# Gated mix of block attention and an MLP: another order of the attention steps, PV groups in pairs on one PSUM tile, and three small moves

## The chip, the cores and the metric

The kernel runs on one core of one Trainium2 chip. The metric is the device time of one execution in microseconds (us). A core has five engines with an instruction queue each: TensorE (PE in the profile, with its weight loads as PEld), VectorE (DVE), ScalarE (ACT), GpSimd (POOL) and SyncE (SP). An engine takes its instructions in the order of its queue and waits at an instruction until the semaphores that it names have been raised by other engines. DMAs are issued here by SP and by ACT, each from its own queue.

## The reference

The function mixes two branches of the same input by a gate per row. S is 2048, D is 512; there are 32 heads of 16 columns; row i sees the keys i-255 to i.

```python
def _A_ref(x, wqkv, wo):                       # H = 32, Dh = 16, W = 256
    q, k, v = split_heads(x @ wqkv)
    scores = jnp.einsum("bhqd,bhkd->bhqk", q, k) * (Dh ** -0.5)
    mask = (idx[:, None] - idx[None, :] >= 0) & (idx[:, None] - idx[None, :] < W)
    p = _softmax(jnp.where(mask[None, None], scores, -1e9), axis=-1)
    o = jnp.einsum("bhqk,bhkd->bhqd", p, v)
    return merge_heads(o) @ wo

def _B_ref(x, w1, b1, w2, b2):                 # F = 1792
    y = _layernorm(x, axis=-1)
    h = _gelu(jnp.einsum("bsd,df->bsf", y, w1) + b1)
    return jnp.einsum("bsf,fd->bsd", h, w2) + b2

x = A_x
g = _sigmoid((x * gate_w).sum(-1, keepdims=True))
return g * _A_ref(x, A_wqkv, A_wo) + (1 - g) * _B_ref(x, B_w1, B_b1, B_w2, B_b2)
```

## The kernel before

Almost every product is made of a high and a low part of each operand (a rounded copy, and what is left after subtracting it): high by high, low by high, high by low. `copy` (L130) makes the high part on ScalarE, `lo_part` (L127) subtracts on VectorE unless told otherwise. The kernel has three stages.

**Projections.** `load_x` (L232) brings four pieces of 512 rows of the transposed input and makes both parts; the piece is c, its four quarters are dt. For the last piece (c = 3) the low parts are made by GpSimd (L250). `qk_unit` (L297) and `v_unit` (L326) make queries, keys and values on TensorE, with twelve matmuls for a unit. Some dozen score steps are done here already, ahead of the attention stage.

**Attention and the first MLP layer, mixed.** The heads are taken in eight groups p of four heads. The program of this stage is written as a string, `ORDER`, of one letter for each step, which `run` (L735) reads:

- `S` (`s_pair`, L348): scores of 128 queries against up to 384 keys for two heads, into a PSUM tile; VectorE masks (L366) and takes the maximum of each row (L367).
- `T` (`st_pair`, L403): the same scores transposed, with the maximum taken off inside the product; ScalarE applies exp (L414), GpSimd cuts the two triangles (L416).
- `P` (`pv`, L423): probabilities times values for 256 queries and four heads, 32 matmul instructions, or 16 for the first of a group p. Here a "full" and a "short" PV group. The sum is copied out of PSUM by ScalarE (`copy`, L441), or by VectorE (L439) once no `S` is left.
- `f` (`fill`, L706): one step of the first MLP layer, a pair of matmuls that run side by side (L638). 24 steps are a unit, whose two halves ScalarE then copies out (`out_half`, L647).

These steps share four PSUM tiles of 128x2x512, b0 to b3, which are handed round: `two` (L112) takes the tile that has been free longest, or another one where the string `PICK` says so. A step that takes a tile waits until the last reader of the tile's previous user has finished.

Every fourth block of queries `put_max` (L371) sends the row maxima through DRAM: GpSimd splits them (step 6 after the last `S`), VectorE transposes them (step 13), `put` stores them to DRAM (step 19, issued by ScalarE; while the projections still run, by SP), and `rest` loads them into the queries' rows (step 28, by SP).

**Second MLP layer and output.** `mlp2(c, f)` (L851) multiplies one of 14 blocks f of the hidden layer for one of four pieces c of rows: 12 matmuls in four groups, one for each 128 rows. Its operand is loaded six items ahead (`load_h`, L689), GELU is applied by ScalarE two items ahead, and VectorE splits it one item ahead (`parts`, L696). `attn_out(c)` (L794) is started at item (0, 4) for c = 0 and at (c-1, 11) for the others: it loads the sums of the softmax, inverts them (`inv`, L809), loads them spread out, and in its later steps scales the attention output (`scale(b)`, b = 0 to 3, VectorE L816, ScalarE, VectorE); one step after each scaling, 12 matmuls apply `wo` (`mm`, L827). `after(k, fn)` (L136) puts a function k items later, at the head of that item.

Of the kernel before, what the change touches and what calls it, by code (L numbers as in the profile page):

```python
# [34 lines left out]
EPS = 1e-5  # L35
NEG = -3.0e38
U8 = mybir.dt.uint8
ORDER = ("TfSfSfffffTfSfffTSfffTfSfffTSfffTfSffSPTSffTfSfffTSfffSPSTfSfffTfSfTffTffTSffTfffTSPSSTPSTfTfffTSffT"
         "ffSffTSffffTSfffTfSffTfSfffSPSTSPTffSTffTfffTfSTffffTSffTfSfffTSfffTfSffSPSSTPTffTSffTffSffTfSfffTSf"
         "ffTfSfffTSfffTfSfSPSTTPTTSPSSTPSffTSffffSTfffTffSffTfSfffTfSffTfSfffSPSTTffffSTffTfffSTffTfffSSPfSfT"  # L40
         "ffSffTfTfffTSPSSTPTffTSfffTfSffTfSffffTSfffTfSffTffSffTPfSSPTffSfTfSffTfSfTffTffSTfffSffTfSfffTSfffS"
         "PTSTPSTSPTffTSffTffSffTSffffTSffffSTfffTffTfSfSfPSSTPfSfTfSfffTfTffSfTfSffffTSfffTfSffffTfSPSTSPTfSf"
         "ffTSfffTfSffTfSfffTfSfTfffTSfTffffTSPTTSPSTSPfTfSTfffSfffTSfffTfSffTfSfffTSfffTfSffSPPSTffTfffSTffTf"
         "ffTfSTfffSfTffTfSffTfSfffSPSSTPSffTfSfffTSfffTfSfffTSfffTfSfffTSffffSPPfSTfTfffSfTffTfSffTffTfSffTff"
         "SfTfTffffSPTTSPSTSPSfffTSfffTfSffTfSffffTSfffTfSffTfSfffSPfSTfTffffTfSTfffTfSfffTSfffTfSffTfSfffSPTS"
         "SPPTSTffffTfSTfffSffTfSfffTSfffTfSffTfffSfSPTSTPSSfTffffTfSffTfSfffTSfffTfSfffTSfffffSTPTTSPTSffTffS"
         "ffTfSfffTSfffTffSfTfTfffSTfTfffSPSSSPPSTSffffTfSfffTSfffTfTfffSTfffTffSTffffSPSTSPSTffTfffSTffTffTSf"
         "ffSffTSfffTfSffTfSfffSPSTSPfTfSTfffTffTSfffTfSfffTSfffTfSffTfSfffSPTTSPSTSPTffTSffTfSfffTfSfffSSfffT"
         "ffffTSffTfSffSPSffTSfffTfSffTfSffSTfffTffTffTfTffffTfPPTTTPfTffTffTffTPPTfTfffTffTfffTTffTfffTfPfTTf"
         "TTffffP")  # L50
PICK = ("0000000000000000001000000000000000000001000100100000000000000000100001000100000000000001000000000000"
        "0000000000000100010000010000000000001001001000101010001000100000000000000000001000000000100000000000"
        "0010000000000001000010020101010000000000100101000000000000000010000001000010000000000000000100100010"
        "1000000000100000000000000000000000000000000000000001000000000000000000010001000000000000001000000100"
        "0000000000000000100000000000000000000000000001001100000010010000000010010000000010000010000000000010"
        "00010000000000000000000101000100000100000000000000010000000000000000000000000000000")
LAG = 6
CHAIN = (6, 13, 19, 28)

# [2 lines left out]
def gated_mix_kernel(ctx, tc: tile.TileContext, xt, x2, wq0, wqk, wv, wo, xa, gw, w1, w2, b1, b2, out):  # L62
    nc = tc.nc
    dve, act, pool, pe, sp = nc.vector, nc.scalar, nc.gpsimd, nc.tensor, nc.sync
# [5 lines left out]
    def nm(s):  # L70
        uid[0] += 1
        return f"{s}_{uid[0]}"
# [30 lines left out]
    def ps(tag, shape=(128, 512)):  # L103
        key, bufs = banks[tag]
        return left[key].tile(list(shape), F32, name=nm("ps_" + tag), tag=tag, bufs=bufs)

    ring, picks = [], list(PICK)

    def choose():
        return ring.pop(int(picks.pop(0)) if picks else 0)  # L110

    def two():  # L112
        if not ring:
            return ps("x", (128, 2, 512))
        ring.append(choose())
        return ps(ring[-1], (128, 2, 512))

    def small(tag, bufs, shape, dt=F32):
        return consts.tile(list(shape), dt, name=nm(tag), tag=tag, bufs=bufs)

    def view(t, *ap, off=0):
        return bass.AP(tensor=t.tensor, offset=t.offset + off, ap=[list(x) for x in ap])

    def f32(t):
        return t.bitcast(F32)

    def lo_part(lo, src, hi, eng=dve):  # L127
        eng.tensor_tensor(out=lo, in0=src, in1=f32(hi), op=ALU.subtract)  # L128

    def copy(dst, src):  # L130
        act.activation(dst, src, AF.Copy)  # L131
# [4 lines left out]
    def after(k, fn):  # L136
        todo.setdefault(step[0] + k, []).append(fn)
# [6 lines left out]
    spot = [None]  # L144
    soons = {}

    def soon(n, fn):
        soons.setdefault(spot[0] + n, []).append(fn)
# [32 lines left out]
    def x8():  # L181
        return get("x", "x8", 10, (128, 2048), F32R)
# [49 lines left out]
    def load_x(c):  # L232
        h, l = x8(), x8()
        xh.append(h)
        xl.append(l)
        raw = vs[:, 4 * c:4 * c + 4].rearrange("p b r -> p (b r)")
        for dt in range(DT):
            sp.dma_start(raw[:, dt * C:(dt + 1) * C], xt[c, :, dt * C:(dt + 1) * C])

        def part(t, dt):  # L240
            return t[:, dt * C:(dt + 1) * C]

        def hi(dt, eng=act):
            if eng is dve:
                dve.tensor_copy(part(h, dt), part(raw, dt))
            else:
                copy(part(h, dt), part(raw, dt))

        def lo(dt):
            lo_part(part(l, dt), part(raw, dt), part(h, dt), dve if c < 3 else pool)  # L250

        def rest():
            for dt in range(DT):
                hi(dt)
                lo(dt)

        return rest, hi, lo
# [113 lines left out]
    def put_max(p, a):  # L371
        mx = mxs[p][:, :, :, a:a + 4]
        m = small("nm", 2, (128, 2, 2, 2, 4), F32R)
        ms = small("ms", 2, (128, 32))
        md = dram.tile([2, 2, 2, 4, 128], F32R, name=nm("md"))

        def parts():
            pool.tensor_copy(m[:, 0], mx)
            lo_part(m[:, 1], mx, m[:, 0], pool)

        def turn():
            dve.transpose(ms, f32(m).rearrange("p a b c d -> p (a b c d)"))

        def put(eng=act):
            eng.dma_start(f32(view(md, [32, 4], [128, 32], [1, 32])), ms)

        def rest():
            done.add(("m", p, a // 4))
            for k in range(2):
                src = view(md, [512, 2], [1024, 2], [1, 512], off=2048 * k)  # L390
                sp.dma_start(f32(qk[62 + k:113 + k:50, :2, a * 128:a * 128 + 512]), f32(src))

        if spot[0] is None:
            parts()
            after(1, lambda: (turn(), put(sp)))
            after(3, rest)
        else:
            for n, fn in zip(CHAIN, (parts, turn, put, rest)):
                soon(n, fn)
# [19 lines left out]
    def flush():  # L419
        while late:  # L420
            late.pop(0)()

    def pv(p, j, last):  # L423
        flush()
        a = two()[:, 0]
        parts = ((-1, 0, 128, 256), (-2, 0, 256, 128), (0, 0, 0, 256), (1, 128, 0, 128))[0 if j else 2:]
        for n, (d, at, fr, w) in enumerate(parts):
            kb = 2 * j + d
            for h in range(4):
                v = (4 * p + h) * VW  # L430
                pe.matmul(a[32 * h:32 * h + 32, at:at + w], vs[:, kb, v:v + 32], pts[p, kb][:, h, fr:fr + w],  # L431
                          start=n == 0, stop=n == len(parts) - 1, skip_group_check=True, tile_position=(0, 32 * h))
        if j % 2 == 0:
            sums.append(sums.pop(0))
            acc[p] = sums[-1]
        s = acc[p]
        o = j % 2 * 256
        if last:
            dve.tensor_copy(s[:, o:o + 256], a[:, :256])  # L439
        else:  # L440
            copy(s[:, o:o + 256], a[:, :256])  # L441
        if j % 2:
            to = osc[p, :, (j - 1) * 256:(j + 1) * 256]
            if lt:
                after(1, lambda: sp.dma_start(to, s))
            else:
                act.dma_start(to, s)
# [287 lines left out]
    def run(order):  # L735
        for a in order:
            spot[0] += 1
            for fn in soons.pop(spot[0], []):
                fn()
            flush()  # L740
            if a == "T":
                p, kb, pr = lt.pop(0)
                if not pr:
                    block(p, kb)
                st_pair(p, kb, pr)
            elif a == "S":
                s_pair(*ls.pop(0))
            elif a == "P":
                pv(*lp.pop(0), not ls)
            else:  # L750
                fill()

    run(ORDER + 6 * "f")
    flush()
# [10 lines left out]
    t = spare[0]  # L765
# [28 lines left out]
    def attn_out(c):  # L794
# [5 lines left out]
        o = get("work", "oa", 2, (128, 4, 512))  # L800
        r = get("work", "ra", 2, (128, 4, 512))
# [42 lines left out]
                after(g, lambda g=g: load_o(g))  # L844
            after(4 + g, lambda g=g: load_r(g))
        for b in range(4):
            after(10 + b, lambda b=b: scale(b, *(t[:, :, b * 128:b * 128 + 128] for t in (o, r))))

    accs = {}

# [30 lines left out]
    for n in range(len(seq)):  # L881
        tick()
        for k in (n + 6,):
            c, f = item(k)
# [4 lines left out]
        c, f = item(n + 1)  # L889
# [6 lines left out]
        c, f = seq[n]  # L896
# [52 lines left out]
```

## Time and profile before

| what | us |
|---|---|
| median of three timed executions | 694.88 |
| lowest and highest of the three | 691.83 and 695.27 |
| the profiled execution, its own time | 691.57 |
| its span, first to last instruction | 689.8 |
| projections (about) | 0 to 144 |
| attention with the first MLP layer (about) | 144 to 488.5 |
| second MLP layer and output (about) | 488.5 to 689.8 |

In the page, a group of instructions stands with its line, its engine, what it writes and reads, how many there are, their busy time and the mean of one. The timeline gives for each piece its start, its length, its engine and, in brackets, how long the engine sat idle before it and who ended that. TensorE's matmuls overlap, so that the end of one lies behind the start of the next: the time that a matmul costs is the distance from its start to the next start, not its length, and a short stall may not show as idle time at all.

### The profile page before, as it was taken

Reading aid. Unit: us, or ns where it says so; the run is one execution under the profiler, and the core shown is the slowest. Engines: PE = TensorE matmul, PEld = TensorE weight load, DVE = VectorE, ACT = ScalarE, POOL = GpSimd, SP = SyncE. Lnnn points to the kernel's source line nnn. Section 1 sums busy time; section 2 is a strip of 40 time slices with the busy share of each in tenths; the row PEclk is TensorE's granted clock in tenths of the full one; section 3 lists DMA queues with packets and bytes.
Section 4 is the critical chain, followed back from the end, with each engine's and each line's share of the span. In section 5 each row is a group of like instructions: output and inputs, shape, how many; then the busy total and the mean of one; then the engine's idle time right before and its main releaser. Section 6 shows DMA issues by size and latency. Waiting matters only on the chain.

```text
span 689.8 us, 15777 instructions
## 1 busy us (share of the span) xinstructions
PE 681.9 (99%) x5738; PEld 538.2 (78%) x5738; DVE 474.1 (69%) x971; ACT 385.5 (56%) x639; POOL 267.2 (39%) x623
## 2 busy tenths in 40 slices
PE   9999999999999999999999999999999999999997
PEld 6887777877877778778787877777787888888886
DVE  6646789966877878778587777866575555556444
ACT  6437454447677676876767767678633224123221
POOL 6900156426566664755666655558000000000000
PEclk9999999999999999999999999999999999999999
DMA  8998888785765668665776556436775450841801
GB/s 319 351 317 271 246 255 270 226 248 176 231 202 165 203 212 271 194 198 177 198 251 195 182 166 202 154 108 216 277 241 189 143 181 4 267 133 40 255 0 62
DMA packets 89621, 137.92 MB, mean 200 GB/s; under 512 B 13160, under 2 KB 36648, under 8 KB 89416
## 3 DMA queue, kind: packets, MB, share of 16 engines
q1 hardware_dynamic: 81120, 128.69, 58.4%
q10 hardware_dynamic: 8424, 8.23, 3.9%
q8 instruction: 46, 0.75, 0.5%
q14 instruction: 31, 0.25, 0.1%
HBM read 81.53 MB, written 54.30 MB: 197 GB/s over the span
## 4 chain that ended last, share of the span: by engine, by line
PE 86%; DMA 7%; POOL 3%; DVE 1%; ACT 1%; SPq 1%; issue 1%; ACTq 0%; DVEq 0%; POOLq 0%
PE ps_b L638 22%; PE ps_a L858 16%; PE ps_b L431 12%; PE ps_d L303 10%; PE ps_b L357 7%; PE ps_b L412 6%; PE ps_o L827 6%; PE ps_d L333 6%; DMA ra<-rd 1%; DMA hp<-t 1%; DMA t<-in_w 1%; DMA oa<-osc 1%; PE ps_x L357 1%; DMA wv<-in_wq 1%; POOL x L128 1%
## 5 line engine op out<-in xcount | busy, mean ns | idle before, releaser
L638 PE MATMUL ps_b<-x,w 64*128 64x512 f32 x1344 | 211.1, 395 | 0.2 <-ACT pb L414 0.2
L858 PE MATMUL ps_a<-x,t 128*128 128x512 f32 x648 | 149.6, 389 | 0.0
L367 DVE TENSOR_REDUCE mx<-ps_b 128x2 f32<-128x512 f32 x208 | 144.1, 693 | 7.2
L858 PEld LDWEIGHTS ps_a<-x,t 128*128 128x128 f32 x648 | 121.6, 188 | 25.3
L638 PEld LDWEIGHTS ps_b<-x,w 64*128 64x128 f32 x1344 | 130.0, 186 | 10.6 <-issue 2.0
L366 DVE COPY_PREDICATED ps_b<-tri,ps_b 128x256 f32<-128x256 uint8 x208 | 88.3, 424 | 44.0 <-PE ps_b L357 32.7
L416 POOL TENSOR_SCALAR_AFFINE_SELECT pa<-pa 128x256 f32<-128x256 f32 x192 | 73.9, 412 | 68.6 <-ACT pa L414 67.9
L414 ACT ACTIVATE pa<-ps_b 128x768 f32<-128x768 f32 x96 | 76.5, 813 | 25.6 <-PE ps_b L412 18.8
L412 PE MATMUL ps_b<-qk 64*128 64x384 f32 (+5 forms) x512 | 88.8, 336 | 0.4 <-ACT pb L414 0.3
L303 PE MATMUL ps_d<-x,w 128*128 128x512 f32 x360 | 85.1, 391 | 0.1
L357 PE MATMUL ps_b<-qk 62*128 62x384 f32 (+3 forms) x472 | 83.2, 345 | 0.8 <-ACT t L131 0.6
L303 PEld LDWEIGHTS ps_d<-x,w 128*128 128x128 f32 x360 | 67.2, 188 | 15.1 <-POOL x L128 0.5
L416 POOL TENSOR_SCALAR_AFFINE_SELECT pb<-pb 128x256 f32<-128x256 f32 x160 | 62.4, 417 | 39.2 <-ACT pb L414 38.5
L414 ACT ACTIVATE pb<-ps_b 128x768 f32<-128x768 f32 (+2 forms) x96 | 65.6, 706 | 16.8 <-PE ps_b L412 12.5
L412 PEld LDWEIGHTS ps_b<-qk 64*128 64x128 f32 (+1 forms) x512 | 50.8, 184 | 15.7 <-issue 4.0
L694 ACT ACTIVATE t<-t,b1s 128x512 f32<-128x512 f32 x56 | 38.5, 716 | 43.4 <-DMA t<-hp 42.8
L416 POOL TENSOR_SCALAR_AFFINE_SELECT x<-x 128x256 f32<-128x256 f32 x128 | 49.7, 417 | 25.8 <-ACT x L414 25.4
L357 PEld LDWEIGHTS ps_b<-qk 62*128 62x128 f32 (+1 forms) x472 | 45.4, 184 | 17.4 <-issue 3.8
L414 ACT ACTIVATE x<-ps_b 128x768 f32<-128x768 f32 x64 | 51.2, 813 | 13.0 <-PE ps_b L412 10.4
L827 PE MATMUL ps_o<-w,t 128*128 128x512 f32 x192 | 46.3, 390 | 1.0 <-ACT t L131 1.0
L333 PE MATMUL ps_d<-wv,x 128*128 128x512 f32 x192 | 46.7, 394 | 0.0
L431 PE MATMUL ps_b<-pa,v 128*32 128x256 f32 (+1 forms) x768 | 43.3, 330 | 0.2 <-POOL x L416 0.2
(96 smaller groups left out, 757.1 us busy)
## 6 DMA issues: line engine op xcount, KB each, us to landing
qk<-qk SPq DMA_DIRECT2D x112, 196.0 KB
t<-hp SPq DMA_DIRECT2D x56, 256.0 KB
hp<-t SPq DMA_DIRECT2D x54, 256.0 KB
qk<-t SPq DMA_DIRECT2D x48, 256.0 KB
osc<-x SPq DMA_DIRECT2D x31, 256.0 KB
t<-in_w SPq DMA_DIRECT2D x28, 256.0 KB
w<-w SPq DMA_DIRECT2D x28, 256.0 KB
qk<-t ACTq DMA_DIRECT2D x24, 256.0 KB
```

Source lines behind the costliest of these rows:

```text
L303: pe.matmul(o, a[:, dt * 128:(dt + 1) * 128], b[:, dt * C:(dt + 1) * C], start=n == 0, stop=n == 11)
L333: pe.matmul(o, x[:, a:a + 128], wvs[dt][:, k], start=n == 0, stop=n == 11)
L357: pe.matmul(o[:, e, :n], qs[pr][r:k, qb * 128:qb * 128 + 128], ks[pr][r:k, t0:t0 + n], start=True, stop=True)
L366: dve.copy_predicated(o[:, :, :128], tri, o[:, :, 256:384])
L367: dve.tensor_reduce(m, o[:, :, :256], mybir.AxisListType.X, ALU.max)
L412: pe.matmul(o[:, e, :w], ks[pr][r:k, kb * 128:kb * 128 + 128], qs[pr][r:k, kb * 128:kb * 128 + w], start=True, stop=True)
L414: act.activation(pt[:, :, :w], o[:, :, :w], AF.Exp, scale=0.25)
L416: pool.affine_select(out=pt[:, :, a:a + 128], in_=pt[:, :, a:a + 128], pattern=[[0, 2], [sgn, 128]], base=b, channel_multiplier=-sgn, comp ...
L431: pe.matmul(a[32 * h:32 * h + 32, at:at + w], vs[:, kb, v:v + 32], pts[p, kb][:, h, fr:fr + w], start=n == 0, stop=n == len(parts) - 1, sk ...
L638: pe.matmul(o[:, e], w[kt // 4][r:r + 64, k, m:m + 128], y[r:r + 64, a:a + C], start=n == 0, stop=n == 23)
L827: pe.matmul(a, x[:, g], wos[g][:, k], start=n == 0, stop=n == 11)
L858: pe.matmul(accs[c][b], x[:, b * 128:(b + 1) * 128], w, start=f == 0 and n == 0, stop=f == FT - 1 and n == 2)
```

## The change

Five things are changed together. The strings `ORDER` and `PICK` are new: the same steps in another order, most of them within a few places of where they were, with the last hundred steps rearranged more. In `pv`, two `P` that follow each other directly now use the two halves of one PSUM tile, where each used to take a tile of its own; any other step closes the pair. The low parts of the last two quarters of the last input piece are made by VectorE instead of GpSimd. The scaling of the first output piece starts 12 items after its start instead of 10. In `put_max`, the stores of the first 99 steps are issued by SP instead of ScalarE.

```diff
-ORDER = ("TfSfSfffffTfSfffTSfffTfSfffTSfffTfSffSPTSffTfSfffTSfffSPSTfSfffTfSfTffTffTSffTfffTSPSSTPSTfTfffTSffT"
+ORDER = ("TfSfSfffffTSffffTSfffTfSfffTSfffTfSffSPTSffTSffTfSffTffSffSPSTfffTSffTffTfSfTfffTfSPSTSPSTfTfffTSfff"
...
         def lo(dt):
-            lo_part(part(l, dt), part(raw, dt), part(h, dt), dve if c < 3 else pool)
+            lo_part(part(l, dt), part(raw, dt), part(h, dt), dve if c < 3 or dt > 1 else pool)
...
-        def put(eng=act):
-            eng.dma_start(f32(view(md, [32, 4], [128, 32], [1, 32])), ms)
+        def put(eng=None):
+            (eng or (act if spot[0] > 99 else sp)).dma_start(f32(view(md, [32, 4], [128, 32], [1, 32])), ms)
...
+    pair = [None]
+
     def pv(p, j, last):
         flush()
-        a = two()[:, 0]
+        if pair[0] is None:
+            pair[0] = two()
+            a = pair[0][:, 0]
+        else:
+            a = pair[0][:, 1]
+            pair[0] = None
...
             flush()
+            if a != "P":
+                pair[0] = None
             if a == "T":
...
-            after(10 + b, lambda b=b: scale(b, *(t[:, :, b * 128:b * 128 + 128] for t in (o, r))))
+            after((10 if c else 12) + b, lambda b=b: scale(b, *(t[:, :, b * 128:b * 128 + 128] for t in (o, r))))
```

The string `ORDER` has 1207 letters before and 1202 after; the five `f` that it lacks follow behind the last `P`. Places where two `P` stand side by side: six before, seven after. Four instructions change their queue besides the two low parts: two stores of maxima go from ACT to SP, and two stores of hidden blocks (`hp<-t`), near the end of the stage, from SP to ACT.

The built programs show where instructions now stand. **TensorE, two PV groups side by side** (steps 584 and 585 in both). Before, the first group writes tile b3 and the second b1; a name's first number is the tile's, the rows are the end of the first group and the start of the second:

```order
L431 MATMUL ps_b3_670_4356<-pa_255_1523,v_4_80 32x128 [waits Pool_49]
L431 MATMUL ps_b3_670_4356<-pa_255_1523,v_4_80 32x128
L431 MATMUL ps_b1_671_4374<-pa_255_1523,v_4_80 32x256 [waits DVE_49,PE_49]
L431 MATMUL ps_b1_671_4374<-pa_255_1523,v_4_80 32x256
L431 MATMUL ps_b1_671_4374<-pa_255_1523,v_4_80 32x256 [waits Pool_49]
```

The same place of the changed program:

```order
L438 MATMUL ps_b0_669_4355<-pa_255_1523,v_4_80 32x128 [waits Pool_49]
L438 MATMUL ps_b0_669_4355<-pa_255_1523,v_4_80 32x128
L438 MATMUL ps_b0_669_4355<-pa_255_1523,v_4_80 32x256 [waits Activation_49]
L438 MATMUL ps_b0_669_4355<-pa_255_1523,v_4_80 32x256
L438 MATMUL ps_b0_669_4355<-pa_255_1523,v_4_80 32x256 [waits Pool_49]
```

Both groups now write the tile b0_669. The second group's first matmul used to wait for VectorE, the last reader of what had been in b1 before; now it waits for ScalarE. By the count that the semaphore must have reached, the instruction waited for is the copy of the first group's sum out of this same tile. So it is in all seven places: five wait for a copy on ScalarE, the last two for one on VectorE.

**ScalarE, the first store of maxima of this stage.** Before (pa and x8 are probabilities, t copies of a finished first-layer unit, md the maxima in DRAM):

```order
L414 ACTIVATE x8_253_1521<-ps_b0_273_1624 128x768
L414 ACTIVATE x8_253_1521<-ps_b3_275_1642 128x768
L385 DMA md_270_1593<-ms_269_1592 4x32x32
L131 ACTIVATE t_277_1660<-ps_b1_261_1536 128x512
L131 ACTIVATE t_278_1662<-ps_b1_261_1536 128x512
L131 ACTIVATE x8_253_1521<-ps_b3_280_1669 128x256
```

After:

```order
L414 ACTIVATE x8_253_1521<-ps_b0_273_1624 128x768
L414 ACTIVATE x8_253_1521<-ps_b3_275_1642 128x768
L131 ACTIVATE t_277_1660<-ps_b1_261_1536 128x512
L131 ACTIVATE t_278_1662<-ps_b1_261_1536 128x512
L131 ACTIVATE x8_253_1521<-ps_b3_280_1669 128x256
```

The store is gone from between the exponentials and the copies of the unit; it stands in SP's queue now.

**TensorE, the first product with `wo`.** Before, it follows the first item of piece c = 1 (written to ps_a_1185 to 1188 with the weights x_1056):

```order
L858 MATMUL ps_a_1187_7877<-x_1056_7104,t_7837 128x512
L858 MATMUL ps_a_1188_7878<-x_1056_7104,t_7836 128x512 x2
L858 MATMUL ps_a_1188_7878<-x_1056_7104,t_7837 128x512
L827 MATMUL ps_o_1191_7897<-w_7303,t_7863 128x512
L827 MATMUL ps_o_1191_7897<-w_7306,t_7863 128x512
```

After (the same four sums are ps_a_1176 to 1179; x_1059 are the weights of the third and fourth item):

```order
L867 MATMUL ps_a_1179_7866<-x_1048_7072,t_7859 128x512
L867 MATMUL ps_a_1176_7863<-x_1059_7161,t_7882 128x512 x2
L867 MATMUL ps_a_1176_7863<-x_1059_7161,t_7883 128x512
L867 MATMUL ps_a_1177_7864<-x_1059_7161,t_7882 128x512 x2
L867 MATMUL ps_a_1177_7864<-x_1059_7161,t_7883 128x512
L867 MATMUL ps_a_1178_7865<-x_1059_7161,t_7882 128x512 x2
L867 MATMUL ps_a_1178_7865<-x_1059_7161,t_7883 128x512
L867 MATMUL ps_a_1179_7866<-x_1059_7161,t_7882 128x512 x2
L867 MATMUL ps_a_1179_7866<-x_1059_7161,t_7883 128x512
L836 MATMUL ps_o_1190_7930<-w_7291,t_7900 128x512
```

Three items of piece c = 1 now stand ahead of the first product with `wo`, where one did.

More of the change, by code (lines that the diff above doesn't have):

```diff
@@ L37 @@
 U8 = mybir.dt.uint8
-ORDER = ("TfSfSfffffTfSfffTSfffTfSfffTSfffTfSffSPTSffTfSfffTSfffSPSTfSfffTfSfTffTffTSffTfffTSPSSTPSTfTfffTSffT"
[L39 to L56, printed above, removed]
+ORDER = ("TfSfSfffffTSffffTSfffTfSfffTSfffTfSffSPTSffTSffTfSffTffSffSPSTfffTSffTffTfSfTfffTfSPSTSPSTfTfffTSfff"
+         "TfSffTfSfffTSfffTfSffTfSfffSPSTSPTffSTffTfffTfSTffffTSffTfSfffTSfffTfSffSPSSTPTffTSffTffSffTfSfffTSf"
+         "ffTfSfffTSfffTfSfSPTSTPTTSPSSTPSffTSffffSTffffTfSffTfSfffTSfffTfSfffSPSTTffffSTfffTffSTffTfffSSPfSfT"
+         "ffSffTfTfffTSPSSTPTffTSffTffSffTfSfffTSfffTfSffTfSffTffSfSPPSTffTfSffTffTSfffTffSfTffSffTfSfffTSfffS"
+         "PTSTPSSTPTffTSffTffSffTfSfffTSfffTfSfffTTfffSfSfPSSTPfTffSTfTffSffTfSfffTSfffTfSfffSTffffTfSPSTSPfTf"
+         "SffTfSfffTSfffTfSfffSfTffTfSfTfffTfSPTSTPSSTPSffTSfffTfTffSfTffSfffTSffffTSfffTffSfSPPTSffSffTffTfff"
+         "STffTfffTfSTffTfSffTfSfffSPSSTPfTfSfffTSfffTfSffTfSfffTSffffSTffffSfSPPfSTfTfffSfTffTfSffTffSffTfffT"
+         "SffTfffTfSPTSTPSSTPSffTfSfffTfSffTfSffffTSfffTfSffTfSfffSPfSTfTffffTfSTfffTfSfffTSfffTfSffTfSfffSPTS"
+         "SPPTSTffffTfSTfffSffTfSfffTSfffTfSffTfffSfSPTSTPSSfTffffTfSffTfSfffTSfffTfSfffSTfffffTSPTTSPTSffTffS"
+         "ffTSffffTSfffTffSfTfTfffSTfTfffSPSSSPPSfTSffffTSfffTfSffTffTffSTfffTffSTffffSPSTSPSTffTfffSTffTffTSf"
+         "ffSffTfSffTfSffTfSfffSPSTSPTffSTffTfffTSffTffSffTSffffTSfffTfSfffSPTSTPSSTPTffTSffTfSfffTfSfffTSfffT"
+         "fSffTfSffTSfffSPSffTSffffTSfffTfSffSfTfffTffTffTPfTfTTffPPTfTfTfffTffTfPfTTPTfTffTfTffTffffTPPTfTfTf"
+         "fT")
@@ new lines @@
+PICK = ("0000000000000000001000000000000000000001001000100000000000000000100001000100000000000001000000000000"
+        "0000000000000100010000010000000000001001001000101010001000100000000000000000000000000000000000000000"
+        "0010000000000000000100201001000000000100100101000000000000000100000001000000010000000000000100100010"
+        "0000000010000000000001000000000000000000010000000100000000000000000010001000000000000000000001000000"
+        "0000000000001000000000100100000000000000010011000000000000000001001000000001000001000000000001000010"
+        "000000000000000000201000100000000000000000000001000000000000000000000000000")
```

## The prediction

> **What bounds the kernel now.** I read the page's busy times first, then the busy time by stage, then the timeline at the places that the change touches.
>
> ```profile
> PE 681.9 (99%) x5738; PEld 538.2 (78%) x5738; DVE 474.1 (69%) x971; ACT 385.5 (56%) x639; POOL 267.2 (39%) x623
> 0.00:143.00 143.00, 141.50 (x619) 110.30 (x620) 103.36 (x196) 73.00 (x157) 57.55 (x71) 1.00 0.87 281
> 143.00:490.00 347.00, 345.48 (x4264) 267.12 (x4263) 261.36 (x589) 250.85 (x386) 209.69 (x552) 1.00 0.62 196
> 490.00:690.00 200.00, 194.94 (x859) 160.77 (x857) 109.36 (x187) 61.62 (x97) 0.00 (x0) 1.00 0.46 148
> ```
>
> The stage rows give length, then the busy time of PE, PEld, DVE, ACT and POOL, and the granted clock. TensorE is the bound in all three stages, at clock 1.00; the next engine, VectorE, is busy 261 of 347 us in the middle one. The change adds or removes no matmul. So what it can move is TensorE's stalls: each microsecond in which it waits is on the path, and work on any other engine counts only through such a wait. What the page calls idle time of TensorE is only about 8 us of the span, since ends are modelled; I measure a stall from start to start. The sum below is made against the profiled execution, 691.57 us (span 689.8 and 1.8 around it), which lies 3.3 under the median of the timed three.
>
> **Pairs of PV groups: a new wait, seven times.** The second group of a pair now waits until the first one's sum is copied out of the shared tile. How long that is, the six old pairs show, where nothing had to wait:
>
> ```profile
> 305.98 0.86 PE L431 MATMUL ps_b<-pb,v 128*32 128x256 f32 x16
> 306.65 1.48 PE L431 MATMUL ps_b<-pa,v 128*32 128x256 f32 x32
> 307.55 0.38 ACT L131 ACTIVATE x<-ps_b 128x256 f32<-128x256 f32 x1 [0.57 <-PE ps_b L431]
> 308.71 0.44 PE L357 MATMUL ps_b<-qk 62*128 62x384 f32 x2
> 328.97 1.51 PE L431 MATMUL ps_b<-pa,v 128*32 128x256 f32 x32
> 329.95 0.38 ACT L131 ACTIVATE x<-ps_b 128x256 f32<-128x256 f32 x1
> 461.58 1.51 PE L431 MATMUL ps_b<-pa,v 128*32 128x256 f32 x32
> 462.50 0.43 DVE L439 COPY x<-ps_b 128x256 f32<-128x256 f32 x1 [1.42 <-PE ps_b L431]
> ```
>
> Sixteen matmuls, half a full group, take 306.65 - 305.98 = 0.67 us from start to start. So at the first place the second group began at 305.98 + 1.34 = 307.32, while the copy of the first ended at 307.55 + 0.38 = 307.93, which is 0.61 later. Behind a short group (16 matmuls) it is 328.97 + 0.67 = 329.64 against 330.33: 0.69, as ScalarE has the two copies of a first-layer unit ahead of it. On VectorE, 462.25 against 462.93: 0.68. From the release to the first matmul I add 0.06:
>
> ```profile
> 152.93 1.05 ACTq L385 DMA_DIRECT2D md<-ms  x1
> 154.08 1.08 ACT L131 ACTIVATE t<-ps_b 128x512 f32<-128x512 f32 x2 [0.87 <-DMA md<-ms]
> 155.22 0.44 PE L357 MATMUL ps_b<-qk 62*128 62x384 f32 x2 [0.60 <-ACT t L131]
> 156.71 0.19 PEld L357 LDWEIGHTS ps_b<-qk 62*128 62x128 f32 x2 [0.45 <-ACT pa L414]
> ```
>
> The copies end at 155.16 and TensorE starts at 155.22. Of the seven pairs three follow a full group with its copy on ScalarE, two follow a short one, two have the copy on VectorE: 3 x 0.67 + 2 x 0.75 + 2 x 0.74 = **+5.0 us**. Nothing hides it: behind the waiting matmul stands TensorE's whole queue, and no later stage of the kernel has slack on TensorE to give back. The lower end for one pair is nothing, were the copy done when the second group comes up, but it reads that group's predecessor; the upper end is one exponential more in front of the copy (0.81 us, below), 1.5. I take the rows, since they are the same two instructions at the same distance.
>
> The Trainium skill ("PSUM — Partial Sum Buffer", Summary: rules for kernel authors) asks to guard PSUM by bank and to read a different bank from the one that matmuls write, and a bank holds 512 fp32 values; the halves of a 128x2x512 tile are then two banks, and by that rule the second group need not wait at all. The built program waits all the same, since it follows the tile. By the rule alone the 5.0 would be nothing, which is the first rival; no run here shows yet which holds.
>
> **Stores of maxima on SP.** In the rows above, ScalarE spends 1.05 us on issuing a store at 152.93 and stands idle 0.87; its copies of the unit come late, TensorE waits 0.60 for them, and 0.45 more for an exponential that is late in turn. Without the store ScalarE goes on when its exponential ends, 0.8 earlier, and the 0.60 goes. The new order has the second of these score steps one first-layer step (0.23) nearer, so of the 0.45 some 0.2 stays. I take **-0.8**; ends 0 and -1.3 (the rows plus the slower restart of the next step, 0.1 each). SP, which now issues the store, is between two loads; behind the store wait the stores of the unit, which no engine needs for long. The second store that moves shows no wait of TensorE: 0.
>
> **End of the stage.** Here tiles come round too fast:
>
> ```profile
> 474.00 0.52 PE L412 MATMUL ps_b<-qk 64*128 64x384 f32 x4
> 474.35 0.65 PE L638 MATMUL ps_b<-x,w 64*128 64x512 f32 x4
> 478.45 0.22 PE L412 MATMUL ps_b<-qk 64*128 64x128 f32 x2
> 479.01 0.33 PE L412 MATMUL ps_b<-qk 64*128 64x128 f32 x2 [0.34 <-ACT pb L414]
> 479.50 1.20 PE L638 MATMUL ps_b<-x,w 64*128 64x512 f32 x8 [0.16 <-ACT pb L414]
> ```
>
> Two pairs of 384 columns take 474.35 - 474.00 = 0.35, so one of 128 columns takes about 0.06. The two at the bottom take 0.56 and 0.49: 0.93 lost on exponentials. The new order puts two or more first-layer steps between these score steps, 0.46 or more, and the row of exponentials is over earlier: **-0.9**, ends 0 and -0.93.
>
> **One run of PV groups fewer.** TensorE goes into and out of a run slowly. A pair of 384 columns between steps of its own kind costs 0.17 (half of the 0.35 at 474); beside the run of PV groups at 306 it costs more:
>
> ```profile
> 305.68 0.34 PE L357 MATMUL ps_b<-qk 62*128 62x384 f32 x2
> 308.99 0.34 PE L412 MATMUL ps_b<-qk 64*128 64x384 f32 x2
> ```
>
> The step ahead takes 305.98 - 305.68 = 0.30, the one behind 308.99 - 308.71 = 0.28: 0.1 each, and as much at the exit itself. There are 58 runs before and 57 after: **-0.3**, ends 0 and -0.4.
>
> **Scaling two items later.** The largest single stall:
>
> ```profile
> 525.75 0.36 DVE L698 CAST t<-t 128x512 fp32r<-128x512 f32 x1
> 526.76 2.48 DVE L866 TENSOR_TENSOR us<-ps_a,b2s 128x512 f32<-128x512 f32 x4
> 529.15 0.69 DVE L816 TENSOR_TENSOR oa<-oa,ra 128x512 f32<-128x512 f32 x1
> 530.62 1.65 PE L827 MATMUL ps_o<-w,t 128*128 128x512 f32 x6 [1.00 <-ACT t L131]
> 533.47 0.84 PE L858 MATMUL ps_a<-x,t 128*128 128x512 f32 x3
> ```
>
> The product with `wo` waits for the scaling, which VectorE reaches only behind the four sums of L866. With the change an item of the second layer stands there instead, and what is late next is its operand, made by the same VectorE behind the same four sums: cast done at 529.24 + 0.42, low part 0.69 later, against a TensorE free at 529.6 and needing the low part 0.46 into the item. Some 0.35 of the 1.00 stays: **-0.65**, ends 0 and -1.2 (the stall with the restart of the next matmuls). The next item's operand is done long before its 2.72 us are over, and the scalings then find VectorE free.
>
> **Low parts on VectorE.** GpSimd's four take 5.49 us from 25.09, and TensorE runs into the last:
>
> ```profile
> 25.09 5.49 POOL L128 TENSOR_TENSOR x<-v,x 128x512 fp32r<-128x512 f32 x4 [1.11 <-ACT x L131]
> 28.71 0.72 DVE L128 TENSOR_TENSOR w<-t,w 128x512 fp32r<-128x512 f32 x1 [3.10 <-ACT w L131]
> 30.64 1.01 PEld L303 LDWEIGHTS ps_d<-x,w 128*128 128x128 f32 x5 [0.55 <-POOL x L128]
> ```
>
> VectorE is idle 3.10 us just there, room for two low parts of 0.69, and GpSimd's remaining two end at 27.8. The idle weight load of 0.55 costs TensorE less than that, since matmuls are under way: **-0.3**, ends 0 and -0.5. The Trainium skill ("SBUF — State Buffer", SBUF: two separate sides) has GpSimd and a VectorE operation with two SBUF inputs lock each other out. By it VectorE's two would end behind GpSimd's, at about 29.2, still ahead of 30.6; the sum stays, and only a later weight part would show it.
>
> **The rest of the order.** Steps are moved by a few places, and I counted the matmul time between a tile's last write and its next user: the old order has 11 of 255 tiles of `T` under 1.0 us and the new one 12, and tiles of `S` under 1.4 us are 14 and 13. Such reuses cost up to 0.2 each in the old trace; I take 0, ends -1 and +1.
>
> **The sum.** 5.0 - 0.8 - 0.9 - 0.3 - 0.65 - 0.3 = **+2.05 us**, so 693.6 for an execution like the profiled one. The kernel's four executions lie at 691.57, 691.83, 694.88 and 695.27, in the middle 693.36; the same kernel spreads over 3.7 us, so I add the change to the middle: **695.4 us**, 0.3% slower.
>
> **Rivals.**
>
> *The pair's wait costs nothing* (the copy comes soon enough, or the rows above mislead): then only the gains are left, 693.36 - 2.95 = 690.4, or 688.0 with every gain at its far end (1.3 + 0.93 + 0.4 + 1.2 + 0.5 and the order's 1, in all 5.3). For it: the halves are separate memory. Against it: the wait is in the program and the copy needs the whole first group. Chance 0.13, half of it (0.06) beyond 0.5% faster.
>
> *The gains don't come.* The stalls of one place reappear at the next, as ScalarE's queue stays full and VectorE stays late: 693.36 + 5.0 = 698.4. For it: TensorE keeps four tiles in flight and each is reused within 1.1 to 1.5 us. Against it: the three stalls each have one plain cause that is taken away. Chance 0.16.
>
> *Copies queue behind exponentials.* On ScalarE a pair's copy can stand behind an exponential that is not done when the PV group ends:
>
> ```profile
> ACT x L131 <- PE ps_b L431: 27.3, 39, 1.8
> 309.43 0.81 ACT L414 ACTIVATE pb<-ps_b 128x768 f32<-128x768 f32 x1
> ```
>
> Then five pairs cost 1.5 and not 0.7: 693.36 + 2.05 + 4 = 699.4. It decides above 0.93 us a pair, where the total passes +3.5. Against it stands the first row: ScalarE waited for the PV group in 39 of 56 copies, so it was there first. Chance 0.08.
>
> The forecast itself has 0.63; it spreads from -0.5 to +3.5 us about the middle of before.
>
> **How the numbers follow.** 0.5% (3.5 us) is about what a measurement of this kernel can tell from no change. Faster by more: half of the first rival, 0.06. Slower by more: the last two rivals and nothing of the forecast, 0.24. Within 0.5%: 0.70. The range reaches from 690.5 (the first rival's usual value) to 699.5 (the third's); beyond either end about 0.1 is left.
>
> **What would show it.** In the changed profile TensorE or its weight loads should sit idle at a PV line behind ScalarE's copy, five times about 0.7, and twice behind VectorE's; the row of PV matmuls (x32) should have a gap in its middle. The idle 0.87 behind the store of maxima, the 0.34 at the last score steps, and the 1.00 at the first product with `wo` should be gone or small. If the pairs show no gap, the first rival holds; if a gap is over 0.9, the third; if the total is over +3.5 with gaps of 0.7, the gains failed.

## The result and the profile after

The changed kernel takes 697.82 us (median of 16 executions, 695.93 to 701.08) against 692.72 (16 executions, 690.27 to 695.34) of the kernel before: a ratio of 1.0075, 95% interval 1.0059 to 1.0091, so 0.75% or 5.2 us slower. The execution that was profiled took 696.19, 4.62 more than the one of before (691.57). TensorE's work is the same, as the head of the page and its first part (busy time, share of the span, instructions) say; what grew is the time between its matmuls.

```profile
span 694.4 us, 15787 instructions
...
PE 681.6 (98%) x5738; PEld 537.7 (77%) x5738; DVE 474.3 (68%) x973; ACT 386.3 (56%) x639; POOL 263.8 (38%) x621
```

The view of one line, of the matmuls of a PV group in the changed kernel (engine, tile, total us and number of times):

```profile
its engine sat idle before it (us, times) until:
  ACT x L131: 2.7, 5
  DVE x L446: 1.1, 2
  POOL x L416: 0.2, 1
  ACT pb L414: 0.2, 1
```

Before the change the same view names only GpSimd, 0.2 once. So the seven pairs wait as the semaphores said, five for ScalarE's copy and two for VectorE's (the last two rows are single waits at other PV groups). One of them in the timeline:

```profile
308.20 0.86 PE L438 MATMUL ps_b<-pb,v 128*32 128x256 f32 x16
308.87 0.83 PE L438 MATMUL ps_b<-pa,v 128*32 128x256 f32 x16
...
309.77 0.38 ACT L131 ACTIVATE x<-ps_b 128x256 f32<-128x256 f32 x1 [0.56 <-PE ps_b L438]
...
310.21 0.86 PE L438 MATMUL ps_b<-pa,v 128*32 128x256 f32 x16 [0.50 <-ACT x L131]
```

The first group should be over, start to start, at 308.20 + 2 x 0.67 = 309.54; the second begins at 310.21, 0.67 later, though the profile calls only 0.50 of that idle. Measured in this way the seven waits are 0.67 to 0.82 and together 5.0 us.

Four stalls of before are smaller or gone. At the store of maxima 0.30 of TensorE's idle time is left where 0.60 stood (155.47), since the store now goes by SP, and the second wait of that place, 0.26 from start to start, is gone. TensorE no longer waits at 30.6 for GpSimd's last low part. At the end of the stage the two short score steps follow each other 0.57 apart with first-layer work between them, and one wait of 0.15 is left. And where TensorE stood 1.00 before the first product with `wo`, it runs through (59 matmuls of the second layer in one row):

```profile
155.47 0.44 PE L357 MATMUL ps_b<-qk 62*128 62x384 f32 x2 [0.30 <-ACT pa L414]
...
485.95 0.24 PE L412 MATMUL ps_b<-qk 64*128 64x128 f32 x2
486.01 0.69 PE L645 MATMUL ps_b<-x,w 64*128 64x512 f32 x4
486.52 0.24 PE L412 MATMUL ps_b<-qk 64*128 64x128 f32 x2
486.58 1.62 PE L645 MATMUL ps_b<-x,w 64*128 64x512 f32 x12
...
488.36 0.64 PE L438 MATMUL ps_b<-x,v 128*32 128x256 f32 x8 [0.15 <-ACT pb L414]
...
526.66 13.60 PE L867 MATMUL ps_a<-x,t 128*128 128x512 f32 x59
```

Three stalls are new, and all lie on the way of the row maxima through DRAM:

```profile
250.21 0.53 ACTq L385 DMA_DIRECT2D md<-ms  x1
...
250.84 1.51 ACT L414 ACTIVATE pb<-ps_b 128x768 f32<-128x768 f32 x2 [1.69 <-DVE mx L363]
...
251.71 0.44 PE L357 MATMUL ps_b<-qk 62*128 62x384 f32 x2 [1.08 <-ACT pb L414]
...
273.11 0.53 ACTq L385 DMA_DIRECT2D md<-ms  x1
...
277.86 1.28 SPq L391 DMA_DIRECT2D qk<-md  x2
...
279.15 0.38 PE L357 MATMUL ps_b<-qk 62*128 62x384 f32 x2
...
280.69 0.45 PE L412 MATMUL ps_b<-qk 64*128 64x384 f32 x2 [1.15 <-DMA qk<-md]
```

The step that waits at 280.69 had no wait in the kernel before, where the load was issued at 275.88:

```profile
275.88 1.28 SPq L391 DMA_DIRECT2D qk<-md  x2
...
278.49 1.11 PE L638 MATMUL ps_b<-x,w 64*128 64x512 f32 x8
...
279.42 0.36 PE L412 MATMUL ps_b<-qk 64*128 64x384 f32 x2
```

At 279 the transposed scores need maxima that were stored at 273.11 and read back by a load issued only at 277.86. TensorE has gone through everything ahead of them at 279.3 and starts at 280.69. The view of the transposed scores (L412) has such waits twice, the second near 455; before, that view names no load at all:

```profile
  DMA qk<-md: 1.5, 2
```

At 250 it is ScalarE that stands for 1.69 at its store, and TensorE 1.08 behind it. These three are 1.1, 1.15 and 0.4 of idle time, some 3.2 us counted from start to start.

### The profile page after: what moved, and what is told of

It reads as the page before. It is cut to its first block, busy times and chain, and to the rows that moved or that the text cites. A ratio compares the mean times of both kernels' runs of the same rounds, so it can differ in the third digit from the quotient of the medians.

```text
span 694.4 us, 15787 instructions
## 1 busy us (share of the span) xinstructions
PE 681.6 (98%) x5738; PEld 537.7 (77%) x5738; DVE 474.3 (68%) x973; ACT 386.3 (56%) x639; POOL 263.8 (38%) x621
## 3 DMA queue, kind: packets, MB, share of 16 engines
q10 hardware_dynamic: 8448, 8.72, 4.2%
## 4 chain that ended last, share of the span: by engine, by line
PE 93%; DMA 2%; ACT 2%; POOL 1%; DVE 1%; issue 1%; SPq 0%; DVEq 0%; ACTq 0%; POOLq 0%
PE ps_a L867 22%; PE ps_b L645 20%; PE ps_b L438 12%; PE ps_d L303 12%; PE ps_d L333 6%; PE ps_b L412 6%; PE ps_o L836 6%; PE ps_b L357 6%; DMA md<-ms 1%; PE ps_d L290 1%; PE ps_x L357 1%; DMA wv<-in_wq 1%; DMA qk<-md 1%; ACT pb L414 0%; ACT t L131 0%
## 5 line engine op out<-in xcount | busy, mean ns | idle before, releaser
L412 PE MATMUL ps_b<-qk 64*128 64x384 f32 (+5 forms) x512 | 89.9, 339 | 1.5 <-DMA qk<-md 1.5
L412 PEld LDWEIGHTS ps_b<-qk 64*128 64x128 f32 (+1 forms) x512 | 51.1, 184 | 18.9 <-issue 5.4
```

Source lines behind the costliest of these rows:

```text
L412: pe.matmul(o[:, e, :w], ks[pr][r:k, kb * 128:kb * 128 + 128], qs[pr][r:k, kb * 128:kb * 128 + w], start=True, stop=True)
```

## The experiments

All ratios are to the kernel before in the same series; 0.1% is 0.7 us. The kernel before had a median of 693.07 in the series of e1 to e4, 693.29 in that of e6 to e9 and 694.03 in that of e10 to e13, so medians of different series can't be set against each other. Nor is a ratio the quotient of two medians; the two can differ by 0.1%.

**The pairs.** The changed kernel with a tile for each PV group again, the kernel before with the pairing alone, and both with the first copy moved behind the second group.

```diff
# e1: the changed kernel, second P of a pair
-            a = pair[0][:, 1]
             pair[0] = None
+            ring.append(ring.pop(0))
+            a = ps(ring[-1], (128, 2, 512))[:, 0]
# e3: the changed kernel; "more" is true where another P follows
+        while outs:
+            outs.pop(0)()
+        outs.append(out)          # out: the copy of this group's sum, and its store
+        if not more:
+            outs.pop(0)()
```

The second, e2, puts the new `pv` into the kernel before, whose order has six adjacent pairs (and skips the entry of `PICK` for the second group, which takes no tile now); e12 is e2 with the copy moved as in e3.

> The changed kernel, but every PV group has a PSUM tile of its own again. Theory A (the seven waits for a copy out of the shared tile are the cost, 5.5 us from their start-to-start gaps of 0.74 to 0.89, and the new order adds stalls of about 3 us on loads of maxima at 250, 279 and 455): 692.4, ratio to before about 1.000, no gap inside the pairs. Theory B (the waits are the cost, and the three new stalls are chance of one execution): 689.5, ratio 0.995. Theory C (the waits are absorbed, the new order itself is slower): 697, ratio 1.006.

> The kernel before with nothing changed but the pairing: its six pairs of adjacent PV groups share a tile. Theories A and B: six waits of about 0.75, so +4.5 us, ratio 1.0065, each seen as idle time of TensorE behind a copy. Theory C: no change, ratio 1.000.

> The changed kernel, with pairs kept, but the copy of a pair's first sum is issued behind the second group's matmuls. Theories A and B: the second group has nothing to wait for, the seven gaps go, -5.4 us against the changed kernel, less about 0.1 a pair because the tile comes free later: 692.5 to 693 with A, 690 with B. Rival: the copies come late for the next users of the tile or for the sums' stores, and half of it comes back: 695.

> The kernel before with only the pairing, and the copy of a pair's first sum behind the second group's matmuls. If the wait for that copy is all that a pair costs: no gap at the six pairs, the time of the kernel before, 693, ratio 1.000. If sharing a tile costs by itself, as it comes free a whole group later: +1 to +2, ratio 1.002.

| kernel | median us | ratio (95%) |
|---|---|---|
| changed | 697.82 | 1.0075 (1.0059 to 1.0091) |
| e1, changed without pairs | 694.66 | 1.0020 (0.9998 to 1.0041) |
| e3, changed, copy behind | 695.84 | 1.0037 (1.0017 to 1.0057) |
| e2, before with pairs | 697.26 | 1.0055 (1.0035 to 1.0075) |
| e12, before with pairs, copy behind | 693.79 | 1.0002 (0.9987 to 1.0017) |

The pairing alone costs 0.55%, 3.8 us (2.4 to 5.2), and in e12, without the wait, the cost is gone within the noise (-0.9 to +1.2 us). In the timelines of e2, and of e12 below it, the same pair:

```profile
307.33 0.86 PE L439 MATMUL ps_b<-pb,v 128*32 128x256 f32 x16
308.00 0.83 PE L439 MATMUL ps_b<-pa,v 128*32 128x256 f32 x16
...
308.90 0.38 ACT L131 ACTIVATE x<-ps_b 128x256 f32<-128x256 f32 x1 [0.56 <-PE ps_b L439]
...
309.34 0.86 PE L439 MATMUL ps_b<-pa,v 128*32 128x256 f32 x16 [0.50 <-ACT x L131]
```

```profile
308.41 0.86 PE L439 MATMUL ps_b<-pb,v 128*32 128x256 f32 x16
...
309.08 1.48 PE L439 MATMUL ps_b<-pa,v 128*32 128x256 f32 x32
310.38 0.61 PE L439 MATMUL ps_b<-x,v 128*32 128x256 f32 x8
310.81 0.40 PE L439 MATMUL ps_b<-pa,v 128*32 128x128 f32 x8
...
311.28 0.39 ACT L131 ACTIVATE x<-ps_b 128x256 f32<-128x256 f32 x1 [1.86 <-PE ps_b L439]
```

In e12 the second half of the first group and the first half of the second are one row of 32 matmuls: nothing waits, in the same shared tile. So neither sharing a tile nor freeing it a group later costs anything that the times can tell; only reading one half between the writes of the two does. One small wait in e12's trace goes with the later copies: behind one pair, after three score steps, comes a third PV group, before which TensorE stands idle 0.25 for VectorE's copy (467.55). The Trainium skill ("PSUM — Partial Sum Buffer", Summary: rules for kernel authors) would have allowed the second group at once, as the halves are two banks; the built program's wait decides, and the trace shows it. e3's seven pairs have no gap, but its time of 695.84 is where the rival on reuse of the tile stood (695) and not where theory A did (692.5 to 693). Time alone does not decide between them, as the intervals of e1 and e3 overlap. The rest of the change costs 0.2% in e1 (-0.02 to 0.41%). Theories B (0.995) and C (1.006) lie outside this interval; A's 1.000 lies at its lower end, so A had the kind of the cost but, if anything, too little of it. Even with no pair, the gains do not appear in the time.

**The small moves alone, and the order in two parts.** e4 is the kernel before with the stores on SP, the two low parts on VectorE and the later scaling. e6 and e7 add to it the new order for steps 1 to 800 or from 801 on (there both orders have made the same steps), with no pairs.

```diff
# e4
-            lo_part(part(l, dt), part(raw, dt), part(h, dt), dve if c < 3 else pool)
+            lo_part(part(l, dt), part(raw, dt), part(h, dt), dve if c < 3 or dt > 1 else pool)
-        def put(eng=act):
+        def put(eng=None):             # act if spot[0] > 99 else sp
-            after(10 + b, lambda b=b: scale(b, ...
+            after((10 if c else 12) + b, lambda b=b: scale(b, ...
# e6, e7: ORDER = new[:800] + old[800:], ORDER = old[:800] + new[800:], PICK cut at the same step
```

> The kernel before with only the three small moves (stores of maxima on SP, two late low parts on VectorE, scaling of the first piece two items later), old order and no pairs. By the stalls that are gone in the changed kernel's trace: -0.6 at 154, -1.2 at 530, -0.5 at 30, together -2.3 us, ratio 0.9967. Rival: the stalls come back a step later, ratio 1.000.

> The three small moves, no pairs, the new order for steps 1 to 800 and the old one behind. Theory S (the new order costs through row maxima that come back from DRAM too late: in matmul time from the store to the first step that needs it, 7.93 before and 6.75 now at the place near 279 us): a stall of 1.3 or more near 279 as in the three kernels with the new order, so +1.0 to +1.5 against the kernel with the small moves alone, 693.5, ratio 1.0005; none near 455 and 473. Rival R (the cost of the new order is spread over many reuses of tiles): +1.9, ratio 1.0005 too, but with no single stall over 1 near 279.

> The three small moves, no pairs, the old order for steps 1 to 800 and the new one behind. Theory S: no stall over 1 near 279; stalls of 0.5 to 0.9 for maxima near 455 or 473 (5.66 us of matmul time from store to need, 8.72 before), and the old stalls of 0.5 and 0.4 near 480 gone: about the same as with the small moves alone, 692.3, ratio 0.998. Rival R: +0.9, ratio 0.999.

| kernel | median us | ratio (95%) |
|---|---|---|
| e4, small moves | 692.34 | 0.9979 (0.9962 to 0.9995) |
| e6, and the new order up to step 800 | 693.66 | 1.0014 (0.9998 to 1.0030) |
| e7, and the new order from step 801 on | 692.61 | 0.9993 (0.9975 to 1.0011) |

The small moves gain 0.2% (1.5 us, 0.3 to 2.6; the two medians alone differ by 0.7), and e4 has the lowest ratio of all runs. The new order without pairs (e1) stands 0.4% above it, about 0.35% of it from the first part. So the whole is 0.55 for the pairs (changed against e1), 0.41 for the order (e1 against e4), less 0.21 for the small moves: 0.75%. The parts are steps of one chain of kernels and must add up; each of them is known to some 0.2 or 0.3. In e6 the timeline shows where the order costs:

```profile
279.26 1.28 SPq L391 DMA_DIRECT2D qk<-md  x2
...
279.36 0.38 PE L357 MATMUL ps_b<-qk 62*128 62x384 f32 x2
...
282.13 0.44 PE L412 MATMUL ps_b<-qk 64*128 64x384 f32 x2 [2.39 <-DMA qk<-md]
```

Counted from start to start, this stall is 1.4, 1.3, 1.8 and 2.6 in the four profiled kernels that have the new order there with the old distances (changed, e1, e3, e6), and 0.1, 0.7, none, 0.6 and none in those with the old (before, e2, e4, e7, e12). Each figure is from one execution; e6's ran 2.7 us above its kernel's median. That speaks for theory S (the maxima come back too late) and against R (many small reuses of tiles). From the store's issue to the matmul that needs the maxima it took 7.5 to 8.8 us wherever TensorE waited here for 0.5 or more, in either order (e7 7.74, e2 7.86, changed 7.57, e6 8.82). With the stall taken off, TensorE reaches that matmul 7.2 us after the store's issue in the five with the old order and 6.3 in the four with the new. The interval of e7's time holds what both theories expected; its trace shows the stall for maxima of the second part, 0.5 idle near 470, and no short score steps that wait near 480.

**The chain of the maxima.** If the distance is the cause, moving the chain must make the stall come and go. e8 and e9 move all chains two steps earlier, in the new order without pairs and in the old one; e10 and e11 move one single chain.

```diff
# e8 (on e1), e9 (on e4)
-CHAIN = (6, 13, 19, 28)
+CHAIN = (4, 11, 17, 26)
# e10 (on e6): this chain alone earlier; e11 (on e4): (6, 13, 23, 32), later
-            for n, fn in zip(CHAIN, (parts, turn, put, rest)):
+            for n, fn in zip((4, 10, 15, 24) if (p, a) == (3, 4) else CHAIN, (parts, turn, put, rest)):
```

> The changed kernel without pairs, with each of the four steps that send the maxima through DRAM two steps (about 0.5 us) earlier: 4, 11, 17, 26 instead of 6, 13, 19, 28. Theory S: the stalls at 279, 455 and 473 shrink by 0.5 each, or go: -1.0 to -1.5 against the same kernel with the old distances (694.7), so 693.4, ratio 1.000. Rival R: no change, 694.7, ratio 1.002, or slower, as GpSimd, VectorE and ScalarE wait for one another at the earlier steps.

> The old order with the three small moves, and the chain of the maxima two steps earlier, as a kernel that may beat both. Theory S: -0.5 against the small moves alone, as its stalls near 214 and 250 shrink: 691.8, ratio 0.997. Rival R: no change, ratio 0.998, or slower by waits at the earlier steps.

> The kernel with the new order for steps 1 to 800 (small moves, no pairs), with one single chain of maxima sent earlier, that of the place near 279 us (steps 4, 10, 15, 24 instead of 6, 13, 19, 28). Theory S: the stall there, 2.6 in that kernel's profile and 1.3 to 1.8 in three others with this order, falls under 0.6; everything else stays: 692.2, ratio 0.999. Rival R: the stall moves on or the time stays, ratio 1.0014.

> The old order with the small moves, and only the chain of the maxima near 279 us later: store at step 23 and load at 32 instead of 19 and 28, so that from the store to the need there is about as little matmul time as in the new order. Theory S: a stall of 1 to 2 near 279 appears, which that kernel lacks: 693.5, ratio 0.9995. Rival R: no stall, ratio 0.998.

| kernel | median us | ratio (95%) | stall near 279, start to start |
|---|---|---|---|
| e8, new order, all earlier | 693.92 | 1.0008 (0.9993 to 1.0022) | none |
| e9, old order, all earlier | 692.62 | 0.9999 (0.9983 to 1.0016) | none |
| e10, new head, one earlier | 692.56 | 0.9988 (0.9969 to 1.0007) | none |
| e11, old order, one later | 692.91 | 0.9987 (0.9968 to 1.0006) | 1.75 |

The stall follows the distance both ways. In the old order it appears when that one chain is made four steps later (e11), and in the new one it goes when it is made four steps earlier (e10, where the load is issued at 274.78 and not at 279.26):

```profile
279.96 1.11 PE L638 MATMUL ps_b<-x,w 64*128 64x512 f32 x8
...
282.64 0.45 PE L412 MATMUL ps_b<-qk 64*128 64x384 f32 x2 [1.57 <-DMA qk<-md]
```

```profile
274.78 1.28 SPq L391 DMA_DIRECT2D qk<-md  x2
...
279.58 0.34 PE L412 MATMUL ps_b<-qk 64*128 64x384 f32 x2
```

Two reservations belong here. In the five profiles with a stall over 1 (changed, e1, e3, e6, e11), SP issues two larger loads of queries and keys (L344, 196 KB each) between the store and the load of the maxima; in the others it issues them behind, except in e8, which has them in between and no stall. So e10 and e11 moved these loads too, and only e8 speaks against them as the cause. And the distance that is enough differs from place to place: near 214 us TensorE needs the maxima 6.3 us after the store's issue in eleven of the fourteen profiles, of both orders. That is as early as near 279 in the new order, yet it waits 0.5 at most, since there they are back within 6.7 us.

In the time the step is at the limit of what can be measured: e10 is 0.26% under e6, about as expected, while e11 is only 0.08% over e4 where 0.15% was expected, and the intervals of each pair overlap. The traces show that TensorE waits at this one place; its share of the 0.4% is not shown. The general remedy failed: e8 gained 0.1% instead of 0.15 to 0.2, and e9 shows no gain (0.9999 for 0.997 expected), though its interval overlaps e4's. In both a stall of 0.5 (start to start) for an exponential stands near 175 that no other kernel has, so moving every chain goes with waits of its own.

**All stores on SP.** In e4's profile a stall near 250 takes 1.4 us from start to start. There ScalarE stands at its store of maxima, which also waits for a semaphore that an earlier transfer of SP raises (L324, a copy within DRAM, issued at 245.31 in e4). e13 is e4 with every store of maxima on SP.

```diff
-            (eng or (act if spot[0] > 99 else sp)).dma_start(...)
+            (eng or sp).dma_start(...)
```

> The old order with the small moves, and all stores of maxima issued by SP, not only the first two. Theory D (part of the gain of the small moves is lost near 250, where ScalarE's store waits for an earlier store of SP that raises the same semaphore, 1.4 in that kernel's profile): the stall near 250 goes, 691.5, ratio 0.997. Rival: SP stands in front of the store longer than ScalarE did, the maxima come later, and stalls for them appear near 214, 279 or 455: ratio 0.999 or more.

e13: 692.57 us, ratio 0.9989 (0.9971 to 1.0008). ScalarE's wait at 250 is gone, but stalls of 1.6 near 259 and 0.8 at 346 (start to start) are there instead, both at the first transposed scores that need a block's maxima. The profile names the load for the second, and VectorE for the first, where the load was issued at 257.49 and the matmul starts at 260.29. The time leans to the rival: 0.999 lies in the interval, and 0.997 just below it. In the trace the stall at 250 went and stalls of the rival's kind came, at other places than it named; e13 is no better than e4.

## Why the prediction was right in its range and short in size

The measured 697.8 lies inside 690.5 to 699.5, and the sign is that of the forecast, but the loss is 5.2 us and not 2.05: beyond the 0.5% to which I gave 0.24. The forecast's own spread ended at +3.5. The range reached 699.5 only for two rivals that did not happen as I described them, so that it holds the result is in part luck.

- **Pairs, +5.0.** Right in place and cause, and in the size of the gaps. I priced 0.67, 0.75 and 0.74; the trace has 0.67 at the pair shown, up to 0.82 elsewhere, 5.0 together. As time, 3.8 were measured for the six pairs of e2, where 4.4 is the sum of their gaps: inside the interval. For the seven of the changed kernel the ratios give 3.8 against e1 and 2.6 against e3, so whether some is given back stays open.
- **Small moves, -0.8, -0.65 and -0.3.** 1.75 forecast, 1.5 measured in e4. The stall at 154 shrank by 0.64, counted from start to start, and that at 30 by 0.29. At 154 I had added 0.45 to the 0.60, but that was idle time of the weight loads; TensorE's matmuls lost 0.26 there. At the scaling, 1.16 went in the changed kernel's profile, where I had left 0.35 for the next operand; e4 shows that rest (0.5 and 0.3), the changed kernel does not. A stall near 250 that I had not seen coming, 0.35 to 1.4, is in nine of the eleven profiles with these moves, and a small one of 0.3 in one of the three without; whether the moves cause it is not settled.
- **End of the stage, -0.9, and one run of PV groups fewer, -0.3.** The stall at 478 did shrink, by 0.6. But these are parts of the order, and the order as a whole did not gain 1.2: it cost 2.8 (e1 against e4, give or take 1.9). No run shows the 0.3 for the run of PV groups by itself.
- **The step that failed is "the rest of the order".** I took 0 with ends -1 and +1, on a count of reuses of PSUM tiles. What the new order shortens is another distance: from the store of a block's maxima to the first transposed scores that need them. Counted in matmul time (the usual start to start of each step), it went by my count of the steps from 7.93 to 6.75 us at the place near 279 and from 8.72 to 5.66 at the one near 455, while the round trip became no shorter: in the changed kernel 4.75 from the store's issue (273.11) to that of the first load (277.86), and 2.8 from there to the matmul (280.69). That one place is worth some 1.5 us on average (1.8 in the four profiles with the new order, 0.3 in the five with the old). The maxima near 455 and 470 add 0.25 to 0.55 and 0.1 to 0.9 in the four profiles that have the new order with the old distances there (changed, e1, e3, e7), and next to none in the others. How the rest of the 2.8 divides, and how much of it is chance, is not settled.
- **Rivals.** The pair's wait did cost (e2, e12), so the first falls. "The gains don't come" gave 698.4, near the measured time, but its mechanism happened only in part: the stalls at 30, 154, 478 and 530 did shrink, and most of the loss came at other places. Some came back near by: in e4 0.8 of the 1.16 at 530, and in e1, e3 and e7 a wait of 0.57 at a PV group near 481 where 0.99 had stood at 478. Copies did not queue behind exponentials: no pair took over 0.93.

The best version found is the old order with the small moves (e4), 0.21% under the kernel before (0.05 to 0.38); e10, e11 and e13 lie within its noise.

## What to carry to other kernels

Where a scheduler follows tiles, two users of the halves of one tile are independent only until one half is read: issue both groups, then both reads. When an order is changed by hand or by search, count every distance that a transfer has to fit in, not only those of the buffers, and set it against the time that the transfer takes at that place; a store and its load moved by four steps were enough to open a stall of 1.75 us (e11). And make such a reordering apart from the moves whose gain is sure, since the sum of both hid that one of them lost.

## What the runs showed of the hardware

The same small round trip through DRAM varies widely. From the issue of the store at 273.11 to the issue of the load at 277.86 took 4.75 us in the changed kernel, of which SP stood 2.8 for the store's landing by the profile; at the same place before it took 3.68:

```profile
272.20 0.52 ACTq L385 DMA_DIRECT2D md<-ms  x1
...
275.88 1.28 SPq L391 DMA_DIRECT2D qk<-md  x2
```

Over all fourteen profiles this time near 279 lies between 3.4 (e10) and 5.9 us (e6), and the stall there between 1.3 and 2.6 in four profiles of the same order. That may be one source of the 5 us by which single executions of one kernel differ; no run tests it.

A store waited here for a DMA of another engine that has nothing to do with its data. The stall at 250 is put down to VectorE by the profile, whose transpose had ended 1.9 us before the store was issued. ScalarE's store names two semaphores, and the second is one that SP's earlier transfer of L324 raises; that wait ended at 249.87 in the changed kernel, 5.4 us after this transfer was issued at 244.49. In the kernel before the same transfer, issued at 244.53, had landed by 249.06, while ScalarE was still at an exponential (until 249.81), and no time was lost. The last 0.3 us up to the issue at 250.21 are not explained.
